# Shifted low words through a PSUM buffer of the up-projection, and x's split on ScalarE and GpSimd in every chunk

## The chip, the cores and the metric

The kernel runs on one core of a Trainium2 chip. A core has five engines with instruction queues of their own: TensorE (PE in the profile, PEld for its weight loads), VectorE (DVE), ScalarE (ACT), GpSimd (POOL) and SyncE (SP), which only starts DMAs here. Each engine runs its queue in order. They meet through semaphores. The metric is the device time of one execution in microseconds, median of several runs.

## The reference

Attention over eight batches with eight heads each, in a causal window of 128 positions with a linear bias, and behind it a two-layer network with a GELU approximation over all 4608 tokens:

```python
scores = scale * np.matmul(q, k.transpose(0, 1, 3, 2)) + bias   # outside the window: -1e9
attn = softmax(scores); attn_out = np.matmul(attn, v)            # (8, 8, 576, 64)
x = attn_out.transpose(0, 2, 1, 3).reshape(4608, 512)
h = x @ w_in                                                     # (4608, 2048)
g = h * (1.0 / (1.0 + np.exp(-1.702 * h)))
return g @ w_out                                                 # (4608, 512)
```

## The kernel before

Every fp32 operand of the network is held as a high part (rounded to the matmul type fp32r) and a low part (the rest), and a product is made of three matmul passes: high by high, high by low, low by high.

**Attention** runs in units of 128 to 256 query rows of a pair of heads. A call of `tick` issues one stage of several neighbouring units: scores on PE (`s_ps`, `sb_ps`), bias and row minimum on VectorE (L369, L380), exponentials on ScalarE (L392, L399, each followed by the reading of its sum), normalisation (L417 on ScalarE, L420 on GpSimd or VectorE, L424), transposition on PE (`t_ps`) and back to SBUF (L446, L474), and the product with v (`x_ps`). Its results gather in four tiles `xf`, one for each chunk of 256 tokens.

**The network** runs over chunks of 256 tokens as a list of jobs: chunk 0 with the first 8 of the 16 slices of the hidden dimension, then chunk 1, then the other half of chunk 0, then chunks 2 to 11, each with all 16 slices. A step is one slice f. `Job.up` makes h in a buffer of PSUM named `h_ps`, of which there are two (12 matmuls, L580), then tanh on ScalarE (L585), g on VectorE (L586, which reads h a last time and so frees its buffer), the high part of g on ScalarE (L589) and the low part on GpSimd (L590). `Job.down` adds g times `w_out` to two accumulators (6 matmuls, L600). `begin` starts a job: `split_x` (L560) makes `xh` and `xl` from x in four pieces k; there is one buffer for each, so the pieces of the next job wait for the last up-projection of this one. In the program the up-projection of a step stands ahead of the down-projection of the step before it. Chunks 12 to 17 are worked on behind this list, in pairs, with seven products in place of eight; nothing there is touched by the change.

**Weights** come from memory as 64-bit words, one 128x512 tile for a slice of `w_in` (w1) and one for `w_out` (w2), so 32 halves. `decode` makes fp32 words of one half: ScalarE converts the upper 32-bit words into the tile `c` (L227), VectorE shifts the lower words right by 29 in place (L228), VectorE joins both (L229), ScalarE writes the high part (L232), GpSimd the low part (L233). Three halves are decoded ahead of the first job; the others are called one to three at a time, ahead of the step that needs them. `c` comes from a pool of five buffers that the output tiles and the sums of weights (`sums`, L650) for chunks 12 to 17 use as well.

**Order.** The program is written in Python order, and a scheduler puts the instructions of each engine into a fixed order ahead of the run. It may move an instruction forward as far as its inputs and buffers allow. The first eight decodings and the transfers of SyncE keep their program order.

Of the kernel before, what the change touches and what calls it, by code (L numbers as in the profile page):

```python
# [8 lines left out]
F32 = mybir.dt.float32  # L9
F32R = mybir.dt.float32r  # L10
BF16 = mybir.dt.bfloat16
I32 = mybir.dt.int32
I64 = mybir.dt.int64
AF = mybir.ActivationFunctionType
ALU = mybir.AluOpType
# [5 lines left out]
P = 128  # L21
# [12 lines left out]
BIG = 3.0e38  # L34
FAR = 1.0e37
DEPTH = 3
BESIDE = range(4)
WB = 2
DECODE_TICKS = 5, 6, 7
FETCH_AHEAD = 6  # L40
# [113 lines left out]
def tile_kernel(ctx: ExitStack, tc: tile.TileContext, q0, k0, v0, qT, kT, v, w_in, w_out, out):  # L154
    nc = tc.nc
# [6 lines left out]
    ps = ctx.enter_context(tc.tile_pool(name="ps", bufs=1, space=PSUM))  # L162
# [56 lines left out]
    def decode(st, name, pin=lambda ins: ins):  # L219

        words = st.bitcast(I32).rearrange("p (m two) -> p m two", two=2)
        top, low = words[..., 1], words[..., 0]
        c = ffn.tile([P, 512], I32, name="wc", tag="o", bufs=OBUFS)

        pin(nc.scalar.activation(c.bitcast(F32), top.bitcast(F32), AF.Prelu, scale=2.0 ** -112, alpha=2.0 ** 32))  # L227
        pin(nc.vector.tensor_scalar(low, low, 29, None, ALU.logical_shift_right))  # L228
        pin(nc.vector.scalar_tensor_tensor(c, c, 3, low, ALU.logical_shift_left, ALU.bitwise_or))  # L229
        w = c.bitcast(F32)  # L230
        res = const.tile([P, 2, 512], F32R, name=name, tag=name)
        pin(nc.scalar.copy(res[:, 0], w))  # L232
        pin(nc.gpsimd.tensor_tensor(res[:, 1], w, res[:, 0].bitcast(F32), ALU.subtract))  # L233
        if name.startswith("w1"):
            kept[name] = w
        return res
# [323 lines left out]
    def split_x(c, x):  # L560
        xh = xp.tile([P, NC, T], F32R, name="xh")
        xl = xp.tile([P, NC, T], F32R, name="xl")
        for k in range(NC):
            (nc.scalar.copy if c in BESIDE else nc.vector.tensor_copy)(xh[:, k], x[:, k])  # L564
            sub = nc.vector if k % 2 else nc.gpsimd
            sub.tensor_tensor(xl[:, k], x[:, k], xh[:, k].bitcast(F32), ALU.subtract)  # L566
        return xh, xl

    class Job:
# [287 lines left out]
    def decode_next():  # L857
        nonlocal halves
        g, ws = halves // 2, (w1, w2)[halves % 2]

        pin = [tc.keep_in_program_order] if halves < PINNED else []
        ws[g] = decode(ws[g], f"w{1 + halves % 2}_{g}", *pin)
        halves += 1
        if ws is w1 and g >= F0 and g % 2:
            sums(g // 2, kept.pop(f"w1_{g - 1}"), kept.pop(f"w1_{g}"))
# [34 lines left out]
    def begin(j):  # L900
        nonlocal seen
        recall(j.c)
        x = xf.pop(j.c)
        j.xh, j.xl = split_x(j.c, x)
        if j.f1 < NF:
            xf[j.c] = x
            send(j.c)
        seen = max(seen, j.c)
        recall(seen + 1)
        j.up(j.f0)  # L910
# [130 lines left out]
```

## Time and profile before

| | us |
|---|---|
| median of 3 runs (1058.39 to 1060.15) | 1059.15 |
| the profiled execution | 1062.32 |
| its span | 1060.5 |
| PE busy | 1037.9 |
| VectorE, ScalarE, GpSimd busy | 683.0, 675.4, 620.1 |

The profile describes one execution. Its own time is 1062.32 us, 1.8 us above the span of its instructions; the median of the other runs is 3.2 us lower. A row of a view names line, engine, operation and tiles, `out<-in`, with counts, busy time and the mean of one instruction. A row of the timeline begins with start and length in us; where the engine sat idle ahead of it, brackets at its end hold the time and what ended it. The windows give the busy time of each engine in a stretch, the clock that PE was granted (1.00 is full), and the share and rate of the DMAs.

### The profile page before, as it was taken

How to read it: one execution, taken by the hardware profiler on the slowest of the kernel's cores; microseconds unless marked ns; L12 is line 12 of the kernel's file. 1: busy time of each engine (PE TensorE's matmuls, PEld its weight loads, DVE VectorE, ACT ScalarE, POOL GpSimd, SP SyncE). 2: the span in 40 equal slices, each digit the busy share in tenths (PEclk: the TensorE clock that was granted, in tenths of full speed). 3: DMA queues.
4: the chain of work that ended last, by engine and by line, in shares of the span. 5: the costliest groups of instructions: out<-in, count | busy, mean ns of one | idle time of the engine just before them, and what ended most of it. 6: DMA issues, size and time to landing. Idle time of an engine off the chain costs nothing.

```text
span 1060.5 us, 21877 instructions
## 1 busy us (share of the span) xinstructions
PE 1037.9 (98%) x6897; PEld 913.6 (86%) x6897; DVE 683.0 (64%) x2280; ACT 675.4 (64%) x1974; POOL 620.1 (58%) x832
## 2 busy tenths in 40 slices
PE   8889999999999999999999999999999999999998
PEld 5557878789998999999899999999988998898987
DVE  6877576357777787867778686776744345436343
ACT  6968876568777777777777777777633334335332
POOL 3668887457676677767677676766642233215121
PEclk9969999999999999999999999999999999999999
DMA  8975456333224234332423432342174556556551
GB/s 286 371 239 185 147 160 196 108 85 94 80 83 131 82 96 125 112 80 89 141 83 113 119 107 81 106 136 69 57 274 163 170 174 212 179 165 205 188 179 60
DMA packets 120276, 151.91 MB, mean 143 GB/s; under 512 B 40033, under 2 KB 96865, under 8 KB 120161
## 3 DMA queue, kind: packets, MB, share of 16 engines
q1 hardware_dynamic: 114400, 140.55, 42.6%
q10 hardware_dynamic: 5760, 9.96, 2.6%
q8 instruction: 55, 0.90, 0.4%
q14 instruction: 61, 0.49, 0.2%
HBM read 119.01 MB, written 31.46 MB: 142 GB/s over the span
## 4 chain that ended last, share of the span: by engine, by line
PE 79%; DVE 4%; issue 1%; DMA 1%; ACT 1%; POOL 0%; POOLq 0%; ACTq 0%; SPq 0%; DVEq 0%
PE acc L600 21%; PE h_ps L580 21%; PE accs L780 11%; PE X_ps L721 6%; PE s_ps L352 5%; PE x_ps L518 4%; PE Y_ps L721 4%; PE t_ps L461 4%; PE x_ps L495 1%; DVE xf L710 0%; DMA xf<-x 0%; PE t_ps L438 0%; DVE xh L564 0%; DMA part<-wc 0%; DVE xl L566 0%
## 5 line engine op out<-in xcount | busy, mean ns | idle before, releaser
L580 PE MATMUL h_ps<-xh,w 128*128 128x256 f32 x1536 | 251.5, 288 | 8.4 <-DVE g L586 7.5
L580 PEld LDWEIGHTS h_ps<-xh,w 128*128 128x128 f32 x1536 | 213.4, 190 | 26.9 <-issue 7.5
L600 PE MATMUL acc<-w,gh 128*128 128x512 f32 x768 | 220.8, 402 | 0.5 <-ACT g L585 0.4
L590 POOL TENSOR_TENSOR gl<-g,gh 128x256 fp32r<-128x256 f32 x192 | 147.1, 767 | 99.4 <-ACT gh L589 78.0
L733 POOL TENSOR_TENSOR gs<-g,gs 128x512 fp32r<-128x512 f32 x48 | 63.4, 1320 | 168.7 <-PE Y_ps L721 113.8
L780 PE MATMUL accs<-w,gs 128*128 128x512 f32 x576 | 148.3, 393 | 0.3 <-POOL gs L733 0.3
L600 PEld LDWEIGHTS acc<-w,gh 128*128 128x128 f32 x768 | 131.7, 190 | 18.2 <-ACT g L585 0.8
L330 POOL TENSOR_TENSOR K<-rk,K 128x384 fp32r<-128x384 f32 (+1 forms) x120 | 108.8, 907 | 50.7 <-ACT K L328 45.5
L580 PE MATMUL h_ps<-xl,w 128*128 128x256 f32 x768 | 137.2, 284 | 0.2 <-DVE xl L566 0.2
L600 PE MATMUL acc<-w,gl 128*128 128x512 f32 x384 | 127.3, 407 | 1.1 <-POOL gl L590 1.1
L780 PEld LDWEIGHTS accs<-w,gs 128*128 128x128 f32 x576 | 102.2, 189 | 17.7 <-POOL gs L733 0.7
L580 PEld LDWEIGHTS h_ps<-xl,w 128*128 128x128 f32 x768 | 112.4, 191 | 5.2 <-issue 0.6
L399 ACT ACTIVATE pb<-pb,mins 128x256 f32<-128x256 f32 (+2 forms) x216 | 104.6, 486 | 11.6 <-DVE mins L380 11.1
L586 DVE SCALAR_TENSOR_TENSOR g<-g,h_ps 128x256 f32<-128x256 f32 x192 | 79.5, 415 | 49.6 <-ACT g L585 48.1
L589 ACT CAST gh<-g 128x256 fp32r<-128x256 f32 x192 | 77.6, 405 | 50.2 <-DVE g L586 45.4
L585 ACT ACTIVATE g<-h_ps 128x256 f32<-128x256 f32 x192 | 72.7, 380 | 56.1 <-PE h_ps L580 45.9
L380 DVE CUSTOM_DVE_ANT_0 pb<-s_ps,bias 128x256 f32<-128x256 f32 (+3 forms) x240 | 86.0, 380 | 26.9 <-PE s_ps L352 24.7
L424 DVE TENSOR_SCALAR_CACHE_REDUCE pb<-pb,rec 128x256 f32<-128x256 f32 (+2 forms) x216 | 91.0, 454 | 3.2
L329 POOL TENSOR_TENSOR Q<-rq,Q 64x256 fp32r<-64x256 f32 (+1 forms) x120 | 83.0, 691 | 13.6 <-ACT Q L310 3.4
L480 DVE TENSOR_TENSOR pl<-t_ps,ph 128x512 fp32r<-128x512 f32 (+2 forms) x120 | 72.9, 607 | 16.0 <-ACT ph L474 14.1
L461 PE MATMUL t_ps<-ident,pb 128*128 128x128 f32 x408 | 80.8, 272 | 0.5 <-DVE pl L480 0.5
L328 ACT CAST K<-rk 128x384 fp32r<-128x384 f32 (+1 forms) x120 | 56.5, 471 | 29.4 <-PE s_ps L352 23.7
(116 smaller groups left out, 2057.8 us busy)
## 6 DMA issues: line engine op xcount, KB each, us to landing
ring<-part SPq DMA_DIRECT2D x84, 512.0 KB, 3.3
rk<-kT SPq DMA_DIRECT2D x72, 192.0 KB, 2.6
rq<-qT SPq DMA_DIRECT2D x96, 128.0 KB, 2.4
out<-o ACTq DMA_DIRECT2D x34, 256.0 KB, 2.8
rw<-w_in SPq DMA_DIRECT2D x16, 512.0 KB, 6.0
rw<-w_out SPq DMA_DIRECT2D x16, 512.0 KB, 6.8
x<-xf SPq DMA_DIRECT2D x13, 512.0 KB, 3.4
xf<-x SPq DMA_DIRECT2D x13, 512.0 KB, 4.4
```

The lines of the kernel that those rows point to most:

```text
L329: nc.gpsimd.tensor_tensor(Q[D:], rq[D:], Q[D:].bitcast(F32), ALU.subtract)
L330: nc.gpsimd.tensor_tensor(K2, rk, K1.bitcast(F32), ALU.subtract)
L380: nc.vector.tensor_tensor_reduce(b.p[ra:rb, cs:b.end], u.s[ra:rb, e, cs:b.end], bias[head][ra:rb, cs:b.end], -SCALE, BIG, ALU.add, ALU.min ...
L399: nc.scalar.activation(live, live, AF.Exp, bias=u.mins[:b.rows, e:e + 1], scale=-1.0, accum_out=u.sums[:b.rows, e, :1],)
L424: nc.vector.tensor_scalar(live, live, u.rec[:rows, e:e + 1], None, ALU.mult, ALU.add, u.rec[:rows, 2 + e:3 + e])
L461: nc.tensor.transpose(u.t[:c.n, w:w + b.rows], b.p[:b.rows, col:col + c.n], ident[:b.rows, :b.rows])
L580: nc.tensor.matmul(h, w1[f][:, z, k * P:(k + 1) * P], x[:, k], start=(n == 0), stop=(n == len(ops) - 1))
L586: nc.vector.scalar_tensor_tensor(g, g, 1.0, h, ALU.add, ALU.mult)
L590: nc.gpsimd.tensor_tensor(gl, g, gh.bitcast(F32), ALU.subtract)
L600: products.append(nc.tensor.matmul(acc, g[:, t * P:(t + 1) * P], w2[f][:, z], start=(f == self.f0 and n == 0), stop=(f == self.f1 - 1 and ...
L721: nc.tensor.matmul(bank, w[:, z, k * P:(k + 1) * P], x[:, y, k], start=start and i == 0, stop=i == len(ops) - 1, skip_group_check=True)
L780: products.append(nc.tensor.matmul(self.acc[t], g[:, y, t * P:(t + 1) * P], w2[f][:, z], start=(f == 0 and n == 0), stop=(f == NF - 1 and ...
```

## The change

In `decode` the shifted low words are no longer written back over the 64-bit tile but into a new tile `bits`, which takes one of the two `h_ps` buffers of PSUM; the joining instruction reads them from there. So a buffer is taken by a shift and free again after the joining. In `split_x` all four high parts are made by ScalarE and all four low parts by GpSimd. Before, VectorE made the high parts in chunks 4 to 11 (32 copies) and the low parts of k = 1 and 3 in all 13 jobs (26 subtractions).

```diff
-BESIDE = range(4)
@@ decode
         pin(nc.scalar.activation(c.bitcast(F32), top.bitcast(F32), AF.Prelu, scale=2.0 ** -112, alpha=2.0 ** 32))
-        pin(nc.vector.tensor_scalar(low, low, 29, None, ALU.logical_shift_right))
-        pin(nc.vector.scalar_tensor_tensor(c, c, 3, low, ALU.logical_shift_left, ALU.bitwise_or))
+        bits = ps.tile([P, 512], I32, name="bits", tag="h_ps", bufs=2)
+        pin(nc.vector.tensor_scalar(bits, low, 29, None, ALU.logical_shift_right))
+        pin(nc.vector.scalar_tensor_tensor(c, c, 3, bits, ALU.logical_shift_left, ALU.bitwise_or))
@@ split_x
         for k in range(NC):
-            (nc.scalar.copy if c in BESIDE else nc.vector.tensor_copy)(xh[:, k], x[:, k])
-            sub = nc.vector if k % 2 else nc.gpsimd
-            sub.tensor_tensor(xl[:, k], x[:, k], xh[:, k].bitcast(F32), ALU.subtract)
+            nc.scalar.copy(xh[:, k], x[:, k])
+            nc.gpsimd.tensor_tensor(xl[:, k], x[:, k], xh[:, k].bitcast(F32), ALU.subtract)
```

In the changed file the lines from L38 to L227 stand one line higher, and those from L566 on too: L585, L586, L589, L590 of before are L584, L585, L588, L589 there. L228 to L233 keep their numbers.

The scheduler gives both kernels the same numbers of matmuls, in another order. On VectorE, in the middle of the first job, stood before (`rw_8`, `rw_9`, `rw_10` are tiles of weights of slices 8 to 10; `wc` is `c`; L369 with `128x1` or `64x1` is the reading of a row minimum):

```order
L228 TENSOR_SCALAR rw_8_595<-rw_8_595 128x512
L228 TENSOR_SCALAR rw_9_611<-rw_9_611 128x512
L369 ISA pb,mins<-s_ps,bias_77 64x192
L369 ISA mins 64x1
L229 SCALAR_TENSOR_TENSOR wc<-wc,rw_2_236 128x512
L228 TENSOR_SCALAR rw_2_238<-rw_2_238 128x512
L228 TENSOR_SCALAR rw_9_613<-rw_9_613 128x512
L410 TENSOR_REDUCE rec<-totals 128x4
L411 RECIPROCAL rec<-rec 128x4
L228 TENSOR_SCALAR rw_10_657<-rw_10_657 128x512
```

and at the same place of the attention stands now:

```order
L228 TENSOR_SCALAR bits<-rw_2_238 128x512
L369 ISA pb,mins<-sb_ps,bias_78 64x192
L369 ISA mins 64x1
L369 ISA pb,mins<-s_ps,bias_79 64x192
L369 ISA mins 64x1
L229 SCALAR_TENSOR_TENSOR wc<-wc,bits 128x512
L228 TENSOR_SCALAR bits<-rw_3_288 128x512
L410 TENSOR_REDUCE rec<-totals 64x2
L411 RECIPROCAL rec<-rec 64x2
L369 ISA pb,mins<-sb_ps,bias_80 64x192
L369 ISA mins 64x1
L229 SCALAR_TENSOR_TENSOR wc<-wc,bits 128x512
```

Before, shifts of later slices stood far ahead of their joinings; now each shift has its joining one to a few rows behind it, and no shift of a later slice comes between.

On PE, ahead of the second step of the first job (`w_1_551` is the decoded slice 1, `acc` the down-projection, `t_ps` the transpositions), stood before:

```order
L342 MATMUL s_ps<-rk,rq 128x256
L342 MATMUL sb_ps<-rk,rq 128x256
L495 MATMUL x_ps<-pw,VV 64x128
L580 MATMUL h_ps<-xh,w_1_551 128x256 x4
L600 MATMUL acc_649<-w_0_482,gh 128x512
```

and now:

```order
L342 MATMUL sb_ps<-rk,rq 64x192
L438 MATMUL t_ps<-ident,pb 128x128 x8
L342 MATMUL s_ps<-rk,rq 64x192
L342 MATMUL sb_ps<-rk,rq 64x192
L495 MATMUL x_ps<-pw,VV 64x128 x2
L495 MATMUL x_ps<-pw,VV 64x256 x2
L495 MATMUL x_ps<-pw,VV 64x128 x2
L438 MATMUL t_ps<-ident,pb 128x64
L438 MATMUL t_ps<-ident,pb 64x64
L438 MATMUL t_ps<-ident,pb 128x64
L438 MATMUL t_ps<-ident,pb 64x64
L579 MATMUL h_ps<-xh,w_1_554 128x256 x8
```

The up-projection of slice 1 has moved behind the down-projection of slice 0 and behind more than one further stage of the attention (units of 64 rows, which came after it before). By the tiles' places in PSUM, its h takes the buffer that the first half of slice 3 frees at its L229, the last row of the VectorE piece above.

On GpSimd, at the start of the second job (`w_8` and `w_9` are weights), the two rows of `xl` from before

```order
L233 TENSOR_TENSOR w_8_1037<-wc,w_8_1037 128x512
L590 TENSOR_TENSOR gl<-g,gh 128x256
L233 TENSOR_TENSOR w_8_1070<-wc,w_8_1070 128x512
L566 TENSOR_TENSOR xl<-xf,xh 128x256 x2
L233 TENSOR_TENSOR w_9_1107<-wc,w_9_1107 128x512
```

are four in a row now:

```order
L233 TENSOR_TENSOR w_8_1088<-wc,w_8_1088 128x512
L589 TENSOR_TENSOR gl<-g,gh 128x256
L565 TENSOR_TENSOR xl<-xf,xh 128x256 x4
L233 TENSOR_TENSOR w_9_1126<-wc,w_9_1126 128x512
```

## The prediction

> **What bounds the kernel now.** First the page's busy times, then the windows, which cut the span into its stages.
>
> ```profile
> PE 1037.9 (98%) x6897; PEld 913.6 (86%) x6897; DVE 683.0 (64%) x2280; ACT 675.4 (64%) x1974; POOL 620.1 (58%) x832
> core 0: us, PE busy (x) PEld busy (x) DVE busy (x) ACT busy (x) POOL busy (x), PEclk, DMA share, GB/s
> 38.10:94.30 56.20, 47.88 (x269) 33.97 (x266) 49.18 (x101) 42.12 (x128) 41.51 (x36) 0.82 0.80 275
> 94.30:160.00 65.70, 64.38 (x414) 51.99 (x415) 41.88 (x106) 50.82 (x143) 55.46 (x51) 1.00 0.46 147
> 260.00:760.00 500.00, 498.84 (x3510) 459.92 (x3509) 380.50 (x1563) 375.55 (x1158) 353.87 (x562) 1.00 0.35 102
> 760.00:1060.50 300.50, 293.62 (x1836) 263.57 (x1834) 130.82 (x209) 115.69 (x252) 91.01 (x77) 1.00 0.53 174
> 48.00:56.00 8.00, 7.58 (x32) 4.99 (x32) 7.97 (x14) 7.43 (x20) 6.37 (x6) 0.57 1.04 368
> 62.00:80.00 18.00, 12.97 (x58) 9.32 (x57) 12.74 (x23) 8.89 (x26) 11.27 (x10) 0.62 0.64 198
> ```
>
> From 260 us to 760 us PE idles 1.2 us of 500: that part is PE's own work, and nothing that the change does there can bring more than this 1.2 us. Behind 760 us the change does nothing. What can be won lies in the first job, here cut at the high part of its first and of its eighth g:
>
> ```profile
> 38.12 0.41 ACT L589 CAST gh<-g 128x256 fp32r<-128x256 f32 x1
> 94.33 0.43 ACT L589 CAST gh<-g 128x256 fp32r<-128x256 f32 x1
> ```
>
> In these 56.2 us PE idles 8.3 us and runs in part at half clock: the two last windows above cost (1 - 0.57) x 8 = 3.4 and (1 - 0.62) x 18 = 6.8 us of clock. VectorE is busy for 49.2 us, more than any other. The timeline shows the worst place:
>
> ```profile
> 61.67 5.89 DVE L228 TENSOR_SCALAR rw<-rw 128x512 int32<-128x512 int32 x1
> 62.35 4.92 POOL L233 TENSOR_TENSOR w<-wc,w 128x512 fp32r<-128x512 f32 x4
> 67.48 0.41 DVE L586 SCALAR_TENSOR_TENSOR g<-g,h_ps 128x256 f32<-128x256 f32 x1
> 68.04 1.20 PE L580 MATMUL h_ps<-xh,w 128*128 128x256 f32 x4 [5.03 <-DVE g L586]
> 81.74 4.12 DVE L228 TENSOR_SCALAR rw<-rw 128x512 int32<-128x512 int32 x1
> ```
>
> One shift lasts 5.89 us, until GpSimd's run of four subtractions is over. g waits behind it, g holds an `h_ps` buffer, and PE stands for 5.03 us. Another shift lasts 4.12 us. By source line, with shortest, median and longest in ns:
>
> ```profile
> L228 DVE TENSOR_SCALAR rw<-rw x32: 399/427/5895, 19.4 to 95.8; 128x512 int32<-128x512 int32 x32
> L229 DVE SCALAR_TENSOR_TENSOR wc<-wc,rw x32: 674/692/2507, 21.8 to 150.6; 128x512 int32<-128x512 int32 x32
> L586 DVE SCALAR_TENSOR_TENSOR g<-g,h_ps x192: 389/417/423, 36.4 to 799.2; 128x256 f32<-128x256 f32 x192
> L627 DVE TENSOR_SCALAR o<-acc x22: 671/682/692, 163.3 to 802.6; 128x512 f32<-128x512 f32 x22
> L566 DVE TENSOR_TENSOR xl<-xf,xh x26: 396/683/996, 20.4 to 746.6; 128x256 fp32r<-128x256 f32 x26
> ```
>
> The operations with all operands in SBUF (L228, L229, L566) are stretched now and then; those with one operand in PSUM (L586, L627) never, in 214 runs, though they run beside the same GpSimd.
>
> **The decoding.** In the first job the two groups of instructions come to
>
> ```profile
> L228 DVE TENSOR_SCALAR rw<-rw 128x512 int32<-128x512 int32 x22 | 26.2, 1210 | 0.7 <-DMA rw<-w_in 0.7
> L229 DVE SCALAR_TENSOR_TENSOR wc<-wc,rw 128x512 int32<-128x512 int32 x16 | 14.4, 915 | 0.0
> ```
>
> of which 26.2 - 22 x 0.427 = 16.8 and 14.4 - 16 x 0.692 = 3.3 us are stretching. After the change both have one operand in PSUM. A shift into PSUM is not in the trace; I take L627's 0.682 us (same form and size, the other direction). Its bounds are 0.427, the free shift, and 1.21, today's mean with the stretching kept. The joining I take at 0.692 us. The order puts 16 shifts between these points, so 16 x 0.682 + 16 x 0.692 = 22.0 us stand in place of 40.6, and VectorE falls from 49.2 to about 31 us, 33 with the four row minima that the new order adds.
>
> The Trainium skill, "SBUF — State Buffer", section "Who interferes with whom", says that VectorE and GpSimd take a shared pair of ports for a whole instruction, and that a VectorE instruction with at most one SBUF input, outside the modes on two ports, stays clear of it. The unstretched rows of L586 agree; without this rule the upper price of 1.21 us could not be called unlikely, and the sum of this part would be near zero. "VectorE: DVE Perf Modes", section "Why PSUM operands drop a tier", speaks against the change: a PSUM operand takes the shift's faster mode away. That is the 0.255 us that L627 has over 0.427, 8 us of VectorE over 32 shifts, and it is in the sum.
>
> What is late next is ScalarE, with 42.1 us in this stretch. Between the same two instructions the new order gives it four more exponentials and their readings,
>
> ```profile
> L392 ACT ACTIVATE pb<-pb,mins 128x256 f32<-128x256 f32 (+2 forms) x20 | 9.2, 466 | 1.6 <-DVE mins L369 1.6
> L392 ACT ACTIVATION_READ_ACCUMULATOR pb<-pb,mins 128x1 f32 (+1 forms) x20 | 4.0, 198 | 0.0
> 40.00:60.00 20.00, 18.18 (x100) 12.48 (x98) 18.72 (x42) 18.17 (x51) 14.66 (x12) 0.83 1.03 362
> ```
>
> 4 x (0.47 + 0.20) = 2.7 us, the rest evens out: 44.8 us. In the 20 us ahead of the long shift ScalarE was 91% busy; at that share 44.8 us take 49.2, so **7.0 us less** than 56.2. PE needs about 47.9 - 9 = 39 us at full clock and GpSimd 41.5 + 2 x 0.84, so neither is ahead of ScalarE. Bounds: 0, if PE's wait only changes its cause, and 56.2 - 44.8 = 11.4, if ScalarE never waits.
>
> **The buffers.** Up to now the two `h_ps` buffers belonged to h alone. Now a shift waits until g has read the h before it, and the next h waits until the joining is done. Queued behind such a shift on VectorE are g and the row minima. The remaining 13 halves fall into the 16 steps from 94 to 160 us,
>
> ```profile
> L585 ACT ACTIVATE g<-h_ps x16: 357/378/417, 94.6 to 153.6; 128x256 f32<-128x256 f32 x16
> ```
>
> 3.9 us apart, where PE idles only 1.3 us. The buffer is held for 0.682 + 0.692 = 1.37 us, if ScalarE's conversion is ready, and in two steps, 7.9 us, a buffer comes round again: mostly covered by the down-projection and attention. By the tiles' places in PSUM, though, five times in the first 24 steps two successive h take the same buffer, so that PE waits for tanh and g (0.38 + 0.42 us) behind what lies between. I take **+1.5 us**; bounds 0 and 13 x 1.37 = 18, without cover.
>
> **x's split.** One start of a job on chunk 4, and the copy on both engines:
>
> ```profile
> 313.11 1.08 DVE L564 CAST xh<-xf 128x256 fp32r<-128x256 f32 x2
> 314.44 0.69 DVE L564 CAST xh<-xf 128x256 fp32r<-128x256 f32 x2
> 315.80 1.62 POOL L566 TENSOR_TENSOR xl<-xf,xh 128x256 fp32r<-128x256 f32 x2
> 316.24 1.46 DVE L566 TENSOR_TENSOR xl<-xf,xh 128x256 fp32r<-128x256 f32 x2
> L564 DVE CAST xh<-xf x32: 273/294/1241, 313.1 to 745.8; 128x256 fp32r<-128x256 f32 x32
> L564 ACT CAST xh<-xf x20: 388/403/415, 16.1 to 255.1; 128x256 fp32r<-128x256 f32 x20
> L566 POOL TENSOR_TENSOR xl<-xf,xh x26: 726/839/975, 16.6 to 747.1; 128x256 fp32r<-128x256 f32 x26
> ```
>
> From the first copy to the last low part pass 4.6 us today. Four pieces on GpSimd behind one copy on ScalarE take 0.40 + 4 x 0.84 = 3.8 us if GpSimd is free: no later than now, and the scheduler spreads the low passes of the first up-projection over other work. ScalarE gains 32 x 0.40 = 13 us and GpSimd 26 x 0.84 = 22, over some 700 us in which they are 75% and 71% busy; VectorE loses 32 x 0.49 + 26 x 0.69 = 34 us that nobody waits for (PE's idle time of 1.2 us is all there is). The cover is GpSimd's free time: where gl (0.77 us) of the step stands behind the four pieces, the down-projection waits. I take **+0.5 us**, bounds -1.2 and 12 x 0.84 x 2 = 20, two pieces uncovered at each boundary.
>
> **Sum.** -7.0 + 1.5 + 0.5 = -5.0: the span of 1060.5 becomes 1055.5, the profiled execution 1057.3. The median shown lies 3.2 us under that execution's 1062.3, so I name 1054.
>
> **The rivals.**
> *The buffers stall PE (slower).* In the new order the second up-projection of the first job waits for the joining of slice 3. Behind the first gh, ScalarE has to go through 4 conversions, 3 high parts and 7 exponentials with readings until then,
>
> ```profile
> L227 ACT ACTIVATE wc<-rw 128x512 f32<-128x512 f32 x16 | 10.4, 677 | 0.0
> L232 ACT CAST w<-wc 128x512 fp32r<-128x512 f32 x17 | 10.3, 618 | 2.6 <-DVE wc L229 2.4
> ```
>
> 4 x 0.68 + 3 x 0.62 + 7 x 0.66 = 9.2 us, and some copies; PE has 49 matmuls, at 39 us for 269 some 7 us. Before, three short gaps in this place were enough for the low clock from 48 to 56 us:
>
> ```profile
> 45.94 0.73 PE L580 MATMUL h_ps<-xh,w 128*128 128x256 f32 x4 [0.71 <-ACT w L232]
> 47.36 0.44 PE L438 MATMUL t_ps<-ident,pb 128*128 128x128 f32 x2 [0.69 <-POOL pb L420]
> ```
>
> If the gap is 5 us, as at 62 us, idle time and low clock cost 5.0 + 6.8 = 11.8 us; with a half uncovered buffer at each of 13 halves (13 x 0.7 = 9) and the 7.0 won it comes to +14, with one of the two to +2 to +5. It decides from 7 us of new PE idle time and lost clock on. I price it at +6, 1065. For it: h and weights share two buffers in a stage where all engines are busy. Against it: PE's total work up to the eighth step is 39 us of 56, so early gaps can be made up. The Trainium skill, "TensorE: Matmul & The Clock Gate", section on the HAM clock gate in Part 1, puts the fall to half clock at an idle window of about 3.4 us; the gap of 5.03 us agrees, the short gaps at 46 us don't, so I don't count on short gaps being free.
> *GpSimd is late for gl and the low parts of K.* Then each of 12 boundaries costs about 1 us: -7 + 1.5 + 12 = +6.5, 1066. Against it: 29% of GpSimd is free.
> *The gain is made up elsewhere.* ScalarE's longer list (2.7 us) and waits at the buffers eat the 7 us: 1059, no change.
> *The whole slack goes.* ScalarE runs without a gap and PE loses no clock: -11.4 - 1.3 = -12.7, 1046.
>
> **How the numbers follow.** Forecast 45% (its own range 1048 to 1057), whole slack 12%, no change 15%, buffers 20%, GpSimd 8%. A measurement of this kernel can tell about 0.2%, 2.1 us, from no change: faster 57%, same 15%, slower 28%. The range takes in the whole slack and both slower cases at their prices: 1045 to 1066.
>
> **What would show it.** Right: L228 near 0.68 us with no long run, L229 near 0.69; the eighth gh some 7 us earlier than 94.3; no idle gap of 5 us on PE; VectorE near 33 us in the first job. Wrong: idle time of PE at h whose releaser is g or the joining; a low clock around 40 to 55 us; PE waiting at jobs' starts for `xl` or at the down-projection for gl; a shift into PSUM that still stretches.

## The result, and the profile after

| | before | after |
|---|---|---|
| median, us | 1059.19 (1058.39 to 1060.15, 4 runs) | 1049.39 (1047.22 to 1050.32, 4 runs) |
| ratio to before, 95% interval | | 0.9904 [0.9887, 0.9922] |
| profiled execution / its span, us | 1062.32 / 1060.5 | 1049.44 / 1047.7 |
| mean granted clock in it | 0.988 | 0.995 |

The change makes the kernel 1.0% faster. The forecast was 1054 us with a range of 1045 to 1066: the sign and the range held, but the gain of 9.8 us is about twice the 5.0 us that the sum gave.

The page's busy times of the changed kernel come first, then the same four windows of both kernels (length, then busy time of PE, its weight loads, VectorE, ScalarE and GpSimd, the granted clock, the DMAs' share and rate). After:

```profile
PE 1029.2 (98%) x6897; PEld 907.6 (87%) x6897; DVE 645.8 (62%) x2222; ACT 682.8 (65%) x2006; POOL 620.4 (59%) x858
0.00:40.00 40.00, 35.38 (x242) 23.09 (x243) 26.48 (x111) 30.56 (x97) 19.66 (x32) 1.00 0.91 321
40.00:80.00 40.00, 35.30 (x230) 25.72 (x228) 29.01 (x82) 37.25 (x115) 31.00 (x31) 0.87 1.00 351
80.00:160.00 80.00, 77.65 (x490) 59.85 (x490) 51.55 (x134) 60.58 (x169) 61.26 (x64) 1.00 0.47 148
160.00:1047.70 887.70, 880.88 (x5944) 798.98 (x5940) 538.75 (x1899) 554.37 (x1628) 508.45 (x732) 1.00 0.42 127
```

Before:

```profile
0.00:40.00 40.00, 35.07 (x225) 22.66 (x226) 25.24 (x111) 28.35 (x89) 16.73 (x29) 0.96 0.92 313
40.00:80.00 40.00, 33.16 (x174) 23.09 (x173) 33.43 (x67) 29.06 (x81) 27.93 (x22) 0.74 0.85 286
80.00:160.00 80.00, 77.21 (x498) 61.55 (x497) 56.15 (x135) 61.99 (x184) 67.14 (x63) 1.00 0.50 161
160.00:1060.50 900.50, 892.46 (x6006) 806.31 (x6005) 568.18 (x1969) 555.98 (x1623) 508.33 (x721) 1.00 0.42 128
```

These rows give an account that needs no mark inside the program. PE has the same 6897 matmuls in both kernels, so a span is PE's idle time, plus the clock that it lost (length times one minus the granted clock), plus a rest. The rest is the matmuls themselves at full clock, and waits too short for the trace to show. The lost clock is taken from windows of 20 us. Half clock that falls on idle time of PE counts in both columns (1.0 us before, 1.3 after, up to 1.7 in the runs below), and the rest comes out that much too low.

| us | idle to 160 us | idle behind 160 us | lost clock | rest |
|---|---|---|---|---|
| before | 14.6 | 8.0 | 12.0 | 1025.9 |
| after | 11.7 | 6.8 | 5.2 | 1024.0 |

Of the 12.8 us between the two spans, 6.8 are lost clock, 2.9 idle time in the first 160 us, 1.2 idle time behind it, and 1.9 the rest. The profiled execution of before was one of its poor ones: 46 other executions of that kernel took 1056.5 to 1064.1 us, at granted clocks between 0.987 and 0.997. So part of the 6.8 us belongs to that execution, and the medians are only 9.8 us apart. The granted clock is on record for every execution, to 0.001, which is 1 us here. Span times one minus that clock has a median of 7.4 us over the 46 executions before, and of 5.2 over the four of the changed kernel (5.8 over the four of its repetition e9, below). By these medians some 2 us of the 9.8 are clock, not 6.8.

The two instructions of the decoding by source line (shortest, median and longest in ns), then the high parts of the first and the eighth g, after:

```profile
L228 DVE TENSOR_SCALAR bits<-rw x32: 680/694/697, 18.8 to 130.4; 128x512 int32<-128x512 int32 x32
L229 DVE SCALAR_TENSOR_TENSOR wc<-wc,bits x32: 673/687/690, 21.2 to 136.0; 128x512 int32<-128x512 int32 x32
37.03 0.40 ACT L588 CAST gh<-g 128x256 fp32r<-128x256 f32 x1
83.21 0.40 ACT L588 CAST gh<-g 128x256 fp32r<-128x256 f32 x1
```

None of the 64 instructions is stretched; before, the longest took 5.9 and 2.5 us. The eighth gh comes 11.1 us earlier, and the first job (from the first to the eighth gh) takes 46.2 us in place of 56.2.

PE's timeline around 45 us, the clock behind it, and PE's waits by cause (total, times, longest), after:

```profile
41.85 0.54 PE L342 MATMUL sb_ps<-rk,rq 64*64 64x192 f32 x2 [1.01 <-ACT pw L446]
42.86 1.16 PE L438 MATMUL t_ps<-ident,pb 128*128 128x128 f32 x8 [0.47 <-ACT pw L446]
45.29 0.55 PE L342 MATMUL s_ps<-rk,rq 64*64 64x192 f32 x1 [1.27 <-DMA rk<-k]
...
48.40 1.98 PE L495 MATMUL x_ps<-pw,VV 128*64 128x128 f32 x12 [1.95 <-DMA VV<-v]
50.31 0.69 PE L438 MATMUL t_ps<-ident,pb 64*128 64x64 f32 x4
50.92 2.07 PE L579 MATMUL h_ps<-xh,w 128*128 128x256 f32 x8
46.00:54.00 8.00, 6.05 (x32) 4.50 (x30) 6.81 (x17) 7.25 (x20) 4.22 (x5) 0.50 1.05 362
PE x_ps L495 <- DMA VV<-v: 2.2, 2, 1.9
PE s_ps L342 <- DMA rk<-k: 1.3, 1, 1.3
PE h_ps L579 <- DVE g L585: 1.1, 2, 0.6
PE h_ps L579 <- DVE wc L229: 0.6, 1, 0.6
PE acc L599 <- POOL gl L589: 0.3, 1, 0.3
```

The 5.03 us wait on g is gone. Short gaps at 41 to 48 us go with half the clock from 46 to 54 us, but they end with ScalarE and with two transfers of the attention, not with the shared buffers: the joining (L229) is waited for once, for 0.6 us.

### The profile page after: what moved, and what is told of

Same layout as the page of the kernel before. It is cut to its first block, busy times and chain, and to the rows that moved or that the text cites. A ratio compares the mean times of both kernels' runs of the same rounds, so it can differ in the third digit from the quotient of the medians.

```text
span 1047.7 us, 21887 instructions
## 1 busy us (share of the span) xinstructions
PE 1029.2 (98%) x6897; PEld 907.6 (87%) x6897; DVE 645.8 (62%) x2222; ACT 682.8 (65%) x2006; POOL 620.4 (59%) x858
## 4 chain that ended last, share of the span: by engine, by line
PE 89%; DMA 4%; DVE 3%; ACT 2%; issue 1%; POOL 1%; SPq 0%; POOLq 0%; ACTq 0%; DVEq 0%
PE h_ps L579 24%; PE acc L599 24%; PE accs L779 11%; PE X_ps L720 6%; PE s_ps L352 5%; PE x_ps L518 5%; PE Y_ps L720 4%; PE t_ps L461 4%; PE x_ps L495 2%; PE t_ps L438 1%; DMA VV<-v 1%; PE sb_ps L342 1%; PE s_ps L342 1%; DMA xf<-x 1%; DMA rw<-w_in 1%
## 5 line engine op out<-in xcount | busy, mean ns | idle before, releaser
L579 PE MATMUL h_ps<-xh,w 128*128 128x256 f32 x1536 | 245.6, 285 | 1.9 <-DVE g L585 1.1
L599 PE MATMUL acc<-w,gh 128*128 128x512 f32 x768 | 216.0, 399 | 0.7 <-ACT half L616 0.5
L589 POOL TENSOR_TENSOR gl<-g,gh 128x256 fp32r<-128x256 f32 x192 | 143.5, 748 | 94.8 <-ACT gh L588 74.4
L585 DVE SCALAR_TENSOR_TENSOR g<-g,h_ps 128x256 f32<-128x256 f32 x192 | 80.0, 417 | 63.8 <-ACT g L584 61.5
L584 ACT ACTIVATE g<-h_ps 128x256 f32<-128x256 f32 x192 | 73.0, 381 | 70.4 <-PE h_ps L579 59.9
L588 ACT CAST gh<-g 128x256 fp32r<-128x256 f32 x192 | 77.5, 405 | 40.5 <-DVE g L585 34.0
L380 DVE CUSTOM_DVE_ANT_0 pb<-s_ps,bias 128x256 f32<-128x256 f32 (+3 forms) x240 | 86.1, 380 | 26.4 <-PE s_ps L352 22.8
L461 PE MATMUL t_ps<-ident,pb 128*128 128x128 f32 x408 | 76.4, 272 | 0.0
L352 PE MATMUL s_ps<-K,Q 128*128 128x256 f32 (+1 forms) x432 | 75.6, 287 | 0.0
```

What stands on the lines that cost most here:

```text
L352: nc.tensor.matmul(u.s[:b.rows, e, b.first:b.end], u.Q[:, b.q0 - u.q0:b.q0 - u.q0 + b.rows], k[:, ko:ko + b.end - b.first], start=(z == 0) ...
L380: nc.vector.tensor_tensor_reduce(b.p[ra:rb, cs:b.end], u.s[ra:rb, e, cs:b.end], bias[head][ra:rb, cs:b.end], -SCALE, BIG, ALU.add, ALU.min ...
L461: nc.tensor.transpose(u.t[:c.n, w:w + b.rows], b.p[:b.rows, col:col + c.n], ident[:b.rows, :b.rows])
L579: nc.tensor.matmul(h, w1[f][:, z, k * P:(k + 1) * P], x[:, k], start=(n == 0), stop=(n == len(ops) - 1))
L589: nc.gpsimd.tensor_tensor(gl, g, gh.bitcast(F32), ALU.subtract)
L599: products.append(nc.tensor.matmul(acc, g[:, t * P:(t + 1) * P], w2[f][:, z], start=(f == self.f0 and n == 0), stop=(f == self.f1 - 1 and ...
```

## The experiments

Twelve runs followed, in three groups of four, each group on a chip of its own; e9 is the changed kernel once more, and e12 is e7 once more. All ratios are to the kernel before on the same chip. Four columns are the account above, made from each kernel's profiled execution. The last is the median of the lost clock over all executions; the kernel before had 6.3, 7.4 and 7.4 us on the three chips.

| run | us | ratio, 95% interval | idle to 160 | idle behind | lost clock | rest | lost clock, all |
|---|---|---|---|---|---|---|---|
| e1 decoding alone | 1051.24 | 0.9925 [0.9904, 0.9947] | 10.0 | 8.1 | 3.4 | 1027.9 | 4.2 |
| e2 split alone | 1053.28 | 0.9944 [0.9924, 0.9964] | 15.1 | 5.9 | 5.2 | 1025.2 | 5.3 |
| e3 whole, `bits` among `t_ps` | 1053.07 | 0.9939 [0.9918, 0.9961] | 11.9 | 6.8 | 1.8 | 1030.6 | 2.1 |
| e4 whole, shift kept in SBUF | 1060.56 | 1.0017 [1.0004, 1.0031] | 18.0 | 6.5 | 8.6 | 1026.0 | 9.5 |
| e5 split of chunks 0 to 3 alone | 1059.11 | 1.0002 [0.9992, 1.0012] | 15.4 | 10.0 | 3.4 | 1028.5 | 4.2 |
| e6 split of chunks 4 to 11 alone | 1055.94 | 0.9965 [0.9951, 0.9978] | 16.0 | 6.3 | 7.0 | 1025.0 | 7.4 |
| e7 decoding, split of 4 to 11 | 1047.81 | 0.9894 [0.9880, 0.9908] | 9.5 | 6.7 | 3.4 | 1026.3 | 5.2 |
| e8 whole, words fetched later | 1053.19 | 0.9950 [0.9930, 0.9969] | 13.1 | 6.2 | 3.6 | 1023.6 | 6.3 |
| e9 whole, again | 1048.58 | 0.9897 [0.9882, 0.9912] | 12.0 | 5.9 | 5.2 | 1022.8 | 5.8 |
| e10 decoding, copies of 4 to 11 | 1045.58 | 0.9872 [0.9855, 0.9888] | 8.2 | 7.6 | 3.4 | 1026.7 | 3.7 |
| e11 decoding, low parts of 4 to 11 | 1052.50 | 0.9934 [0.9921, 0.9946] | 8.9 | 9.8 | 3.4 | 1028.8 | 4.2 |
| e12 as e7, again | 1047.73 | 0.9888 [0.9871, 0.9906] | 9.3 | 6.8 | 3.4 | 1026.3 | 4.2 |

### One half of the change at a time

e1 has the new `decode` and the old `split_x`:

```diff
-        pin(nc.vector.tensor_scalar(low, low, 29, None, ALU.logical_shift_right))
-        pin(nc.vector.scalar_tensor_tensor(c, c, 3, low, ALU.logical_shift_left, ALU.bitwise_or))
+        bits = ps.tile([P, 512], I32, name="bits", tag="h_ps", bufs=2)
+        pin(nc.vector.tensor_scalar(bits, low, 29, None, ALU.logical_shift_right))
+        pin(nc.vector.scalar_tensor_tensor(c, c, 3, bits, ALU.logical_shift_left, ALU.bitwise_or))
```

> Only the decoding is changed; x's split is that of before. Theory (the gain is the first job's stretched shifts and joinings): L228 near 0.69 us without long runs, the eighth gh near 83 us as with the whole change (94.3 before), 1048 to 1051 us. Rival (the split brings a part, by freeing VectorE): 1052 to 1056 us, the eighth gh still early but PE idle at starts of jobs.

e2 has the old `decode` and the new `split_x`:

```diff
-            (nc.scalar.copy if c in BESIDE else nc.vector.tensor_copy)(xh[:, k], x[:, k])
-            sub = nc.vector if k % 2 else nc.gpsimd
-            sub.tensor_tensor(xl[:, k], x[:, k], xh[:, k].bitcast(F32), ALU.subtract)
+            nc.scalar.copy(xh[:, k], x[:, k])
+            nc.gpsimd.tensor_tensor(xl[:, k], x[:, k], xh[:, k].bitcast(F32), ALU.subtract)
```

> Only x's split is changed; the shift stays in SBUF. Theory: no gain of the early stage, the long shifts stay, 1058 to 1060 us (PE's idle time in chunks 4 to 11 is 1.2 us in all, so at most that is won). Rival (the split brings a part): 1053 to 1056 us.

The decoding alone gives a ratio of 0.9925, 7.9 us of 1058 (5.6 to 10.2); its time lies just above the theory's range, and its eighth gh comes at 81.96 us. By the table's last column 2.1 us of it are clock. The split alone gives 0.9944, 5.9 us (3.8 to 8.0), of which 1.0 is clock. The second was a miss: the prediction had put the split at +0.5 us. It did not leave the decoding as it was either. By source line, L228 and L229 of e2:

```profile
L228 DVE TENSOR_SCALAR rw<-rw x32: 409/466/1505, 18.8 to 87.4; 128x512 int32<-128x512 int32 x32
L229 DVE SCALAR_TENSOR_TENSOR wc<-wc,rw x32: 660/1172/4955, 21.2 to 141.0; 128x512 int32<-128x512 int32 x32
```

The stretching went from the shift (longest 5.9 us before) to the joining (4.96 us, median 1.17), and PE's idle time to 160 us stayed at 15.1 us. So in the first 160 us e2 wins nothing but clock over the profiled execution of before, which was a poor one; its idle time behind them falls from 8.0 to 5.9 us.

### Is it the stretching, or the order and the buffer?

e4 keeps the new split and was meant to hold an `h_ps` buffer from shift to joining, as the change does. But the work is done in SBUF; only one column of 512 passes through PSUM, in two more VectorE instructions for each half (0.16 us each).

```diff
-        pin(nc.vector.tensor_scalar(bits, low, 29, None, ALU.logical_shift_right))
-        pin(nc.vector.scalar_tensor_tensor(c, c, 3, bits, ALU.logical_shift_left, ALU.bitwise_or))
+        pin(nc.vector.tensor_scalar(low, low, 29, None, ALU.logical_shift_right))
+        pin(nc.vector.tensor_copy(bits[:, :1], low[:, :1]))
+        pin(nc.vector.scalar_tensor_tensor(c[:, :1], c[:, :1], 3, bits[:, :1], ALU.logical_shift_left, ALU.bitwise_or))
+        pin(nc.vector.scalar_tensor_tensor(c[:, 1:], c[:, 1:], 3, low[:, 1:], ALU.logical_shift_left, ALU.bitwise_or))
```

> The shift and the joining stay in SBUF (all but the first of 512 columns), but an h_ps buffer is taken between them as in the changed kernel, so the order is near that of the changed kernel. Two VectorE instructions of one column are added per half. Theory (stretching): L228 and L229 stretch again, beyond 1 us in the mean for L228, the eighth gh not before 91 us, 1056 to 1064 us. Rival (the order: shifts of later slices no longer stand ahead of g): L228 stretches, but the eighth gh comes at 83 to 86 us and the time is 1048 to 1052 us.

The gain is gone: 1.0017, and the eighth gh comes at 90.95 us. VectorE's groups of e4 from 40 to 80 us (busy time and mean ns of one), the large joining by its source line, the window itself, and PE's two largest waits:

```profile
L231 DVE SCALAR_TENSOR_TENSOR wc<-wc,rw 128x511 int32<-128x511 int32 x16 | 20.6, 1293 | 0.1
L228 DVE TENSOR_SCALAR rw<-rw 128x512 int32<-128x512 int32 x18 | 13.7, 768 | 0.0
L229 DVE COPY bits<-rw 128x1 int32<-128x1 int32 x13 | 2.0, 152 | 0.1
L230 DVE SCALAR_TENSOR_TENSOR wc<-wc,bits 128x1 int32<-128x1 int32 x13 | 1.9, 149 | 0.5 <-ACT wc L226 0.3
L231 DVE SCALAR_TENSOR_TENSOR wc<-wc,rw x32: 674/770/3637, 21.9 to 147.8; 128x511 int32<-128x511 int32 x32
40.00:80.00 40.00, 30.80 (x175) 22.29 (x172) 38.91 (x94) 30.95 (x88) 28.88 (x24) 0.83 0.92 308
PE h_ps L581 <- DVE wc L230: 4.1, 2, 3.6
PE t_ps L440 <- POOL pb L422: 3.9, 2, 2.0
```

VectorE is busy for 38.9 of 40 us, where the changed kernel has 29.0. In these 40 us the stretching costs 20.6 - 16 x 0.692 = 9.5 us on the joinings and 13.7 - 18 x 0.427 = 6.0 us on the shifts. The extra one-column instructions cost 3.9 us. The buffer is now held while a joining stretches, so PE waits 3.6 us for it.

But e4 doesn't part the stretching from the order. Its shift needs no buffer; the buffer is taken by the copy behind it (L229). So the scheduler moves the shifts far ahead again: the rows above have 18 shifts and only 13 copies. Counted along VectorE, up to 13 shifted halves wait for their joining in e4, as many as before the change, and at most 2 in the changed kernel. Its order is that of before, and not, as was expected, near that of the changed kernel. It also holds the new split, which alone brought 5.9 us: against e2 on the same chip e4 is 7.3 us slower, 4.2 of them clock.

What the runs do show is that the pass through PSUM ends the stretching. The Trainium skill, "SBUF — State Buffer", section "Who interferes with whom", says that a VectorE instruction with at most one SBUF input, outside the modes on two ports, stays clear of the ports that GpSimd and VectorE share. The runs agree: every shift into PSUM, in all the kernels that have one, stays within 0.71 us, while in SBUF a shift took up to 5.9 us (before) and a joining up to 5.0 (e2). In every run the pass through PSUM and the close order come and go together, so which of them brings the decoding's gain is not shown. VectorE's time speaks for the stretching: by the prediction's rows it cost 20.1 us in the first job, while the new order takes six shifts out of that stretch (16 in place of 22), 6 x 0.43 = 2.6 us. What it is worth to g that no shift of a later slice stands ahead of it, no run tells; a shift in SBUF, kept close to its joining, would.

e3 gives `bits` one of the two `t_ps` buffers (the transpositions') in place of an `h_ps` buffer:

```diff
-        bits = ps.tile([P, 512], I32, name="bits", tag="h_ps", bufs=2)
+        bits = ps.tile([P, 512], I32, name="bits", tag="t_ps", bufs=2)
```

> The whole change, but bits takes a buffer of t_ps (the transpositions') in place of h_ps. Theory: the shift is as short, so the first job is again some 10 us shorter; which buffers it borrows is worth the 2.4 us that PE idles from 83 to 150 us at most: 1047 to 1052 us. Rival (h waiting for weights is what holds the changed kernel back): below 1046 us, if t_ps is the freer pair.

Its shifts are as short as in the change (0.69 us), its eighth gh comes at 77.27 us, 5.9 us ahead of the changed kernel, and it loses the least clock of all (1.8 us). It still takes 1053.1 us, outside both ranges. The loss stands in the rest, 6.6 us above the changed kernel's (5.3 without the half clock that was counted twice). Its 32nd gh is still 5.6 us ahead of the changed kernel's (177.42 and 183.02 us), its 64th 1.6 us behind (311.79 and 310.22). The stages hold different shares of the attention, so this gives no cause, and it stays open. It shows that the `h_ps` buffer is not the worse choice, and that an early eighth gh is no gain by itself.

### Which part of the split brings its share?

On the old decoding, e5 changes the split only for the jobs of chunks 0 to 3 and e6 only for chunks 4 to 11:

```diff
 # e5
-            sub = nc.vector if k % 2 else nc.gpsimd
+            sub = nc.vector if k % 2 and c not in BESIDE else nc.gpsimd
 # e6
-            (nc.scalar.copy if c in BESIDE else nc.vector.tensor_copy)(xh[:, k], x[:, k])
-            sub = nc.vector if k % 2 else nc.gpsimd
+            nc.scalar.copy(xh[:, k], x[:, k])
+            sub = nc.vector if k % 2 and c in BESIDE else nc.gpsimd
```

> Decoding as before; of x's split only the jobs of chunks 0 to 3 are changed (their low parts k = 1 and 3, 10 subtractions, go from VectorE to GpSimd); chunks 4 to 11 as before. The split alone gave 1053.3 us against 1057.9, which the prediction had put at nothing. Theory A, its gain comes from the first jobs, where another order of the decoding follows (eighth high part of g at 88.4 us in place of 94.3): this kernel takes 1052 to 1055 us, the eighth gh near 88 us, and from 260 to 760 us PE idles 1.2 us as before. Theory B, it comes from the jobs' starts in chunks 4 to 11: this kernel stays within 2 us of before, 1056 to 1060 us.

> The counterpart: decoding as before, the split of chunks 4 to 11 alone is changed (32 copies from VectorE to ScalarE, 16 subtractions from VectorE to GpSimd), that of chunks 0 to 3 as before. Theory A: 1056 to 1058 us, the eighth gh at 94 us as before, and only the 1 us of PE's idle time between 260 and 760 us is won. Theory B: 1052 to 1055 us, with PE's idle time between 260 and 760 us gone and the distance from the 112th to the 192nd high part of g some 3 us shorter than the 232.5 us of before.

e5 is no different from before (1.0002), although its eighth gh comes at 87.05 us, 7.3 us earlier. It loses 3.2 us less clock than before (last column) and as much more elsewhere; where isn't shown. e6 has 0.9965, 3.7 us (2.3 to 5.2), none of it clock. Its 1055.94 us lie between the two theories' ranges, but theory B's signs are there: from 260 to 760 us PE doesn't idle at all, and from the 112th to the 192nd gh pass 292.6 us in place of 295.7 (the expectation's 232.5 us run from the 128th). So the gain belongs to the jobs of chunks 4 to 11, the stage in which the prediction had found only 1.2 us to win. On the new decoding, e10 moves only their copies to ScalarE and e11 only their low parts to GpSimd; e7 and e12 move both:

```diff
 # e10
-            (nc.scalar.copy if c in BESIDE else nc.vector.tensor_copy)(xh[:, k], x[:, k])
+            nc.scalar.copy(xh[:, k], x[:, k])
 # e11
-            sub = nc.vector if k % 2 else nc.gpsimd
+            sub = nc.vector if k % 2 and c in BESIDE else nc.gpsimd
```

> Decoding changed, and the split of chunks 4 to 11; the split of chunks 0 to 3 as before. The decoding alone gave 1051.2 us, the whole change 1049.4. If in the whole change the split's gain is that of the later chunks (some 1 to 2 us): 1049 to 1050 us, with the eighth gh near 82 us. If the split in the first jobs is what adds to it: 1051 us, as with the decoding alone. If the early split costs, because it delays the first step of the second job on GpSimd: 1047 to 1048 us, faster than both kernels.

> The whole change as it is, for a comparison on one chip with the three that follow. Both theories: 1048.5 to 1050.5 us.

> Decoding changed; of the split of chunks 4 to 11 only the 32 copies go from VectorE to ScalarE, the low parts stay on both engines, and chunks 0 to 3 are as before. The decoding alone gave 1051.2 us, with the whole late split 1047.8. Theory: at a job's start VectorE has four copies (2.0 us) and two subtractions (1.4 us) more in its queue, and what stands behind them (the attention's pl, g) comes late for PE; the copies are the larger and the earlier part, so this kernel takes 1048 to 1049.5 us, and the waits of PE for pl (0.28 us twice in the trace of the decoding alone) are gone. Rival: the copies were hidden, and it is the low parts k = 1 and 3 that PE waits for: 1050.5 to 1051.5 us.

> The counterpart: decoding changed; of the split of chunks 4 to 11 only the 16 low parts of k = 1 and 3 go from VectorE to GpSimd, the copies stay on VectorE. Theory (VectorE's queue at a job's start, of which the copies are the larger part): 1049.5 to 1051 us. Rival (PE waits for the low parts): 1047.5 to 1049 us.

> Decoding changed, and the split of chunks 4 to 11 alone, once more, beside the whole change on one chip. If the split of chunks 0 to 3 costs the whole change something, this kernel is 1 to 2 us below it (1047 to 1048.5 us); if not, both agree within 0.5 us.

The copies are the gain: e10 (0.9872) lies clear of the decoding alone (0.9925), and of e11 (0.9934). e10 came out better than the theory's 1048 to 1049.5 us and e11 worse than its 1049.5 to 1051; lost clock, 3.7 and 4.2 us, hardly parts them. The low parts bring nothing: e11 does not differ from e1, and e7 and e12, with copies and low parts, come out 2 us above e10, though with intervals that overlap. e7 lies where an early split that costs would put it. e12 is 0.9 us below e9 with largely overlapping intervals, so whether the early low parts cost anything isn't settled; the profiled executions of e7 and e12 show 3.4 us of lost clock, that of e9 5.2.

The account says where. e10 and e11 are alike up to 160 us; the last window of each, e10 first:

```profile
160.00:1045.90 885.90, 878.25 (x5920) 795.64 (x5919) 546.23 (x1913) 556.72 (x1622) 497.50 (x710) 1.00 0.41 127
```

```profile
160.00:1050.90 890.90, 881.13 (x5920) 796.85 (x5919) 550.17 (x1929) 546.78 (x1590) 508.10 (x726) 1.00 0.41 126
```

For the same 5920 recorded matmuls this stage takes 5.0 us longer with the copies on VectorE: 2.1 us are idle time of PE and 2.9 us are "busy" time. Over all kernels, the four that keep the copies on VectorE (before, e1, e5, e11) have 8.0 to 10.0 us of idle time behind 160 us, the ten others 5.9 to 7.6.

Where these 5.0 us lie can be estimated from the starts of the matmuls. Each is charged the median time to the next start that its shape has behind 160 us over all kernels (0.12 us for 256 columns, 0.23 for 512); what a stretch lasts beyond the sum of its charges is delay. In the eight stretches from 1 us ahead of the first copy of a job to 14 us behind it, chunks 4 to 11, e11 has 4.7 us more delay than e10, and in all the rest from 290 to 765 us 0.4 us more. The kernel before has 3.0 and 0.1 us more than e10. So the time is lost at the starts of the jobs.

How a copy on VectorE makes PE late can be seen in the kernel before at the start of a job at 499 us. VectorE's timeline, and below it two pieces of PE's:

```profile
499.39 1.83 DVE L564 CAST xh<-xf 128x256 fp32r<-128x256 f32 x3
501.14 0.15 DVE L411 RECIPROCAL rec<-rec 128x2 f32<-128x2 f32 x1
501.32 0.68 DVE L557 TENSOR_TENSOR xf<-x_ps,xb 64x64 f32<-64x64 f32 x3
502.04 0.84 DVE L564 CAST xh<-xf 128x256 fp32r<-128x256 f32 x1
502.80 0.41 DVE L566 TENSOR_TENSOR xl<-xf,xh 128x256 fp32r<-128x256 f32 x1
...
504.80 0.74 DVE L566 TENSOR_TENSOR xl<-xf,xh 128x256 fp32r<-128x256 f32 x1
505.47 0.41 DVE L380 CUSTOM_DVE_ANT_0 pb<-s_ps,bias 128x256 f32<-128x256 f32 x1
...
508.25 0.68 DVE L480 TENSOR_TENSOR pl<-t_ps,ph 128x512 fp32r<-128x512 f32 x1
```

```profile
311.99 1.07 PE L580 MATMUL h_ps<-xh,w 128*128 128x256 f32 x8
312.90 0.27 PE L461 MATMUL t_ps<-ident,pb 128*128 128x128 f32 x1
...
507.99 0.73 PE L461 MATMUL t_ps<-ident,pb 128*128 128x128 f32 x3
508.99 0.33 PE L461 MATMUL t_ps<-ident,pb 128*128 128x128 f32 x1 [0.27 <-DVE pl L480]
```

VectorE works without a gap of more than 0.05 us from 499.39 to 506.2 us, and 2.67 us of that are copies. They stretch as well: four unstretched copies would take 4 x 0.294 = 1.2 us. The row minima (L380) and, after exponentials and normalisation, pl follow late, and a transposition waits for pl. The idle time shown there is 0.27 us. Yet three transpositions of 128 columns need about 0.17 us from start to start (eight matmuls of 256 columns take 312.90 - 311.99 = 0.91 us from start to start, 0.11 each, and these are half as wide), so the next could have started at 508.16 and started at 508.99: 0.83 us are lost. Not all of it is the wait for pl: the row of three ends at 508.72, and one transposition is recorded with 0.33 us, so the third started at about 508.39 and was late itself. The recorded end of a matmul lies far behind its start (0.33 us for a transposition that holds up the next by 0.06), so short waits vanish in it. This is one place. That the rest of the 2.9 us of "busy" time is made of such waits is argued from it and from where the time is lost, not shown.

### Can the early loss of clock be avoided?

e8 fetches the weights' words 4 slices ahead in place of 6:

```diff
-FETCH_AHEAD = 6
+FETCH_AHEAD = 4
```

> The whole change, but the weights' words are fetched 4 slices ahead of their decoding in place of 6. In the whole change PE waited at 44 to 49 us for two transfers of the attention (1.27 us for rk, 1.95 us for VV) beside DMAs that are busy all the time, and ran at half clock from 46 to 54 us. If the weights' transfers, started too early, are what delays them: these two waits shrink below 0.5 us, the clock of 40 to 60 us rises from 0.74 to over 0.85, and the time falls by 2 to 4 us to 1045 to 1047.5. Rival, the waits are given by the order in which the transfers stand in the queues and not by the share of the weights: the waits stay, 1049 to 1050 us. Third, the words now come late for the shifts (waits of VectorE or ScalarE for the DMA of w_in or w_out of over 2 us): 1051 to 1055 us.

The profiled execution is the fastest of six, 1048.27 us: its waits for rk and VV are 0.6 and 1.0 us (1.3 and 2.2 in the change) and its clock from 40 to 60 us is 0.91, partly as the theory expects. But the other five took 1050.5 to 1056.4 us, with granted clocks down to 0.991, and the median of 1053.2 lies in the third theory's range. No trace of a slower execution exists, so its cause stays open. Fetching later did not help.

## Why the prediction was right or wrong

**The decoding, -7.0 us: right in mechanism, as far as the runs show.** The shift into PSUM takes 0.694 us (taken at 0.682) and is never stretched, as its unstretched neighbours with a PSUM operand suggested, and VectorE is busy 33.97 us in the first job (33 forecast). Whether the end of the stretching or the new order is the gain isn't parted by any run. After the change the first job reads:

```profile
37.03:83.21 46.18, 41.48 (x270) 30.05 (x267) 33.97 (x102) 43.43 (x137) 35.43 (x38) 0.89 0.93 331
```

It became 10.0 us shorter in the profiled pair, not 7.0. ScalarE works 43.4 us at 94% there in place of the forecast 44.8 at 91%. But PE's idle time in it fell only from 8.3 to 4.7 us, and half clock cost up to 10.1 us of it before (0.18 x 56.2) and 5.1 after (0.11 x 46.2), which the step from ScalarE's work to time did not count. So the size is in part luck. And the mark was badly chosen: e5 has its eighth gh 7.3 us early and wins nothing, e3 has it 17.1 us early and wins 6.4. As a gain in time, decoding and buffers together were put at -5.5 us; e1 measured -7.9, and the forecast lies just outside its interval (5.6 to 10.2). Without the 2.1 us of clock it would be -5.8.

**The clock** was priced in the prediction (3.4 and 6.8 us) but not kept as a term of its own. Between the profiled executions it is the largest, 6.8 of 12.8 us; between the medians of all executions it is some 2 us of 9.8.

**The buffers, +1.5 us: not borne out.** The changed kernel idles 2.35 us from 80 to 160 us, but e1, which takes the same buffers with the old split, idles 1.0 (before: 2.8):

```profile
80.00:160.00 80.00, 79.03 (x511) 62.69 (x509) 56.60 (x142) 62.48 (x176) 60.70 (x62) 1.00 0.48 153
```

So the idle time there is not the buffers' price. What shows of them is one wait for the joining, 0.6 us in the changed kernel and 0.9 in e1. The rival in which the buffers stall PE didn't happen, though its sign did: the second up-projection moved to 50.9 us (39.2 before) and the clock was low from 46 to 54 us, but PE was waiting for transfers and ScalarE there.

**x's split, +0.5 us: wrong, and the gain is clear in e6 and e10.** The failed step is the sentence that VectorE loses 34 us "that nobody waits for (PE's idle time of 1.2 us is all there is)". The split alone brings 5.9 us, and on top of the decoding the whole change is 2.2 to 3.0 us below e1 by the ratios, though with intervals that overlap. Moving the copies does it. Two things were read wrongly: a queue 76% busy on average still puts a dense stretch of six instructions in front of pl and g at a job's start; and PE's idle time was taken as the whole of its loss, although its "busy" time holds short waits as well. GpSimd was not late, as said: its low parts even got shorter (0.839 us at the median before):

```profile
L565 POOL TENSOR_TENSOR xl<-xf,xh x52: 723/736/760, 16.4 to 734.1; 128x256 fp32r<-128x256 f32 x52
```

So the miss of 5 us has two parts: by the ratios, some 2.4 us of the decoding with the buffers (-7.9 against -5.5), most of it clock, and 2.7 to 3.5 us of the split (-2.2 to -3.0 against +0.5).

## What to carry to other kernels

Where VectorE and GpSimd work side by side, look at the longest instance of each VectorE instruction with all its operands in SBUF. Passing one operand through PSUM makes a shift 0.27 us longer here (0.694 in place of 0.427) and ended stretching of up to 5.5 us, where a PSUM buffer was free for the 1.4 us. When an experiment is to keep an order, count the order in its trace: e4 did not keep it.

PE's idle time is a lower bound of its loss: compare the length of a stage for the same matmuls, or the starts of two neighbouring matmuls, before saying that nothing is left to win there. Split a change into its parts and run them alone: here one part was worth some us, one nothing, and the version with the copies and without the moved low parts (e10, 1045.6 us, 1.3% below before) came out 3.0 us under the whole change on the same chip, with intervals that overlap slightly; some 2 of the 3.0 us are clock.

## What the hardware showed that was not expected

**The clock falls after several short gaps.** In the changed kernel PE's gaps around the fall at about 45 us were 1.01, 0.47 and 1.27 us, and PE was busy for 1.70 of the 3.41 us ahead of it (41.33 to 44.74). In windows of 1 us the loss is 5.12 us, so 10.2 us of half clock; in e1, e7 and e10 to e12 3.41 (6.8 us), in e3 1.71 (3.4 us). The Trainium skill, "TensorE: Matmul & The Clock Gate", section on the HAM clock gate in Part 1, gives a window of about 3.4 us: these lengths agree with whole windows, one, two and three. Its rule that a whole window must be idle for the fall isn't borne out here, by PE's recorded busy time.

**The same kernel runs at different clocks.** Before had 0.987 to 0.997 over 46 executions, with times of 1056.5 to 1064.1 us, so one profiled execution can carry some us of clock that the median doesn't have.

**Stretching moves.** When only the split changed (e2), the longest shift fell from 5.9 to 1.5 us and the longest joining rose from 2.5 to 5.0. Both long ones had a run of GpSimd's instructions beside them (four L233 to 67.3 us before, three from 77.6 to 81.3 us in e2), so which instruction pays seems to go with what the order puts there.
